# Attention into two gated layers: the power-of-two scale of x1, from Gram matrices of the values or from x1's own maxima per chunk of tokens

## The chip, the cores and the metric

The kernel runs on one core of one Trainium2 chip. A core has a matrix engine (TensorE, in the rows PE for matmuls and PEld for its weight loads), VectorE (DVE), ScalarE (ACT), GpSimd (POOL) and SyncE (SP), which here only issues transfers. Each engine takes its instructions in a fixed order and waits at one until what it needs is there. SBUF is the working memory, PSUM (8 banks) takes the matmul results. The metric is the device time of one execution in microseconds (us), as the median of three runs.

## The reference, cut to what matters

```python
# attention: 2 batches, 8 heads, 576 tokens, head size 64
out_up    = repeat(softmax(scale * mean4(q) @ mean4(k).T) @ mean4(v), 4)   # pooled by 4 tokens
out_local = softmax(scale * q @ k.T where |i - j| < 4) @ v                 # a narrow band
x1 = (out_up + out_local), as 1152 tokens x 512

# first layer, 512 -> 1536 -> 512
x2 = (silu(x1 @ w_gate) * (x1 @ w_val)) @ w_out

# second layer, 8 experts of 512 -> 1024 -> 512, weighted by a balanced routing table
logits = x2 @ moe2_w_gate
P = exp(logits - logits.max());  8 rounds of row and column normalization
out = sum over e of  P[:, e] * (relu(x2 @ w1[e]) @ w2[e])
```

Inputs are float32 and the weights of the first layer come as 64-bit floats that the kernel converts itself. Large products are done in three float16 matmuls each: an operand is scaled by a power of two and split into a high and a low float16 half.

## The kernel before

The work stands in one long program; a scheduler fixes each engine's order before the run, from priorities (mostly the order in which the code is written) and its own idea of durations. It is fully unrolled, so every instruction has one place in its engine's row.

**Attention** (`attention`, L332) goes through 16 heads, two of them (a pair) in one 128-partition tile; pairs 0 to 3 are batch 0, pairs 4 to 7 batch 1. For a head, `scores` (L360) does the score matmuls (tiles `s`, L365 to L374), maxima on DVE (`stm`, `nb`), seven exponentials on ACT (`ex`, L386 to L391) and the division on POOL (L397 to L401); `turn` (L404) transposes on PE (tiles `t`) and copies on ACT (`at`). `combine` (L421) multiplies a pair with its values (tiles `o`, L430 and L438), ACT takes the pooled part out (`avd`, L441), and DVE adds both into `x1` (L444): 128 features x 576 tokens. Scores run four heads ahead of the turns. The tiles `s`, `t` and `o` take two banks each from a ring of six.

**The scale.** x1 is split into `xhl` (high and low half) by `split` (L160): ACT writes the high part, DVE the low part, both times a power of two `s`. Before, `s` is known early: `load_va` (L308) loads a second copy of the values (8 transfers of 288 KB), `x1_scale` (L314) multiplies each 128-column piece with itself on PE (40 matmuls into the tile `vv`), and the largest entry bounds the values. `allmax` with `short` (L153) takes a maximum over the partitions by PE (one transposing matmul), DVE (a reduce) and PE again (a broadcasting matmul, tile `sm`); `pow2` makes the scale in four small DVE operations. Each pair is split in `combine` as soon as its x1 is there.

**First layer.** The 1152 tokens are two chunks, `CH = ((0, 256), (512, 320))`: chunk 0 is tokens 0 to 511 (all of batch 0 but its last 64), chunk 1 is tokens 512 to 1151. For each of 12 blocks f of hidden features, `prep_gv(f)` (L200) loads 1 MB, converts it (`cvg`, L190 to L197), takes its magnitude sum on ACT (L206), its scale by `allmax` (tile `sm_gv`), and splits it into the weight tile `gv`. `gv_step(c, f)` (L487) does the products: for chunk 0 24 matmuls of 512 columns, for chunk 1 48 of 320 columns. For f below 3 on chunk 0 ("early") the results lie in single banks of the pool `psg` (tag `y`, two banks) and pass tanh on ACT and three DVE operations (L515 to L517); later blocks use other banks. The `sm` tiles of `allmax` come from the same two banks, and the two are handed out in the order of the code. Chunk 1 follows chunk 0 by 3 blocks.

`prep_gv(0)` and `prep_gv(1)` are placed among the heads (PREP_AT). From then on each preparation is tied to a step (L640):

```python
with tc.issue_after(gv_done[0, f - 1].ins) if f else nullcontext():
    prep_gv(f + np_)          # np_ = 2
```

so `prep_gv(3)` may not start before the last DVE operation of `gv_step(0, 0)`, `prep_gv(4)` not before that of `gv_step(0, 1)`. Behind the first layer stand `w_out`, the routing and the eight experts (`h_step`, `y_step`), which take most of the run.

Of the kernel before, what the change touches and what calls it, by code (L numbers as in the profile page):

```python
# [22 lines left out]
P = 128  # L23
# [31 lines left out]
@with_exitstack  # L55
def tile_kernel(ctx, tc, qT, kT, vw, vd4, va, wgv, wo, wg2, w1, w2, out):
    nc = tc.nc
# [14 lines left out]
    def tmp(n, nm):  # L72
        return wp.tile([P, 16], F32, tag="tmp", bufs=56, name=nm)[:, :n]
# [86 lines left out]
    def split(hi, lo, src, s, pool=False):  # L160
        if pool:
            A.activation(src, src, AF.Copy, scale=s)
            return A.copy(hi, src), G.tensor_tensor(lo, src, hi, op=ALU.subtract)
        return (A.activation(hi, src, AF.Copy, scale=s),  # L164
                V.scalar_tensor_tensor(lo, src, s, hi, op0=ALU.mult, op1=ALU.subtract))  # L165
# [138 lines left out]

    vas = []
    x1s = []

    def load_va():  # L308
        for i in range(B * NPAIR):
            t = mp.tile([P, 2 * CH[1][1]], F32, tag="xT", bufs=4, name=f"va{i}")[:, :S]  # L310
            nc.sync.dma_start(t, va[i])
            vas.append(t)

    def x1_scale():  # L314


        ps = psg.tile([P, 512], F32, tag="y", name="vv")[:, :P]
        for i, t in enumerate(vas):
            b = t.bitcast(BF16)[:, 1::2]
            for lo in (0, P, 2 * P, 4 * P, 3 * P):  # L320
                n = min(P, S - lo)
                T.matmul(ps[:n, :n], lhsT=b[:, lo:lo + n], rhs=b[:, lo:lo + n],
                         start=(i, lo) == (0, 0), stop=(i, lo) == (B * NPAIR - 1, 3 * P))
        mx = tmp(1, "mxv")
        V.tensor_reduce(mx, ps, axis=AX.X, op=ALU.max)
        m = tmp(1, "mv")
        V.tensor_scalar(m.bitcast(U32), allmax(mx, 1, "v", True).bitcast(U32), 0x7F800000, 1, op0=ALU.bitwise_and,
                        op1=ALU.logical_shift_right)
        V.tensor_scalar(m.bitcast(U32), m.bitcast(U32), float(127 << 22), None, op0=ALU.add)
        x1s.extend(pow2(m, 1, "x1", room=4.0))  # L330

    def attention():  # L332
# [3 lines left out]

        qd, kd, exs, ats = {}, {}, {}, {}

        def pooled(pr):
# [81 lines left out]
        def combine(pr):  # L421
# [21 lines left out]
            for i, (lo, hi) in enumerate(((0, base), (base, S))):  # L443
# [3 lines left out]
                                op=ALU.add)  # L447
            b, k = pr // NPAIR, pr % NPAIR
            o = slice(b * S, (b + 1) * S)
            split(xhl[:, 0, k, o], xhl[:, 1, k, o], x1, x1s[0])  # L450

# [10 lines left out]
        for h in range(AHEAD):  # L462
            start(h)
            if h == 1:
                pooled_v(0)
                x1_scale()
            yield
# [19 lines left out]
    def gv_step(c, f, early):  # L487
# [4 lines left out]
        with tc.high_priority():  # L492
            V.tensor_scalar(iv[:, 0:1], gv_inv[f], x1s[1], 0.5 if early else 1.0, op0=ALU.mult, op1=ALU.mult)
            if early:
                V.tensor_scalar(iv[:, 1:2], iv[:, 0:1], 2.0, None, op0=ALU.mult)
# [135 lines left out]
    load_v(1)  # L631
    load_va()
    for n, _ in enumerate(attention()):
# [148 lines left out]

_INS = ("qT", "kT", "vw", "vd4", "va", "wgv", "wo", "wg2", "w1", "w2")

# [37 lines left out]
```

## Time and profile before

| | us |
|---|---|
| median of 3 runs | 1054.92 |
| lowest and highest | 1052.87, 1056.31 |
| the profiled execution | 1055.02 |
| its span in the trace | 1053.2 |
| PE busy in the span | 1019.6 (97%) |
| DVE, ACT, POOL busy | 767.7, 450.1, 94.3 |

The profile is of one execution, 1.8 us longer than its span and 0.1 us above the median. Times in the trace count from the span's start. The part with attention ends at about 127 us (the last `o` matmul), the first layer follows, and from there to the end PE is the busy engine. A row of a busy table gives time in which an engine worked; what decides the end is the chain of waits, which the profile follows back from the last instruction.

### The profile page before, as it was taken

The numbers are of one execution on the slowest core, as the hardware profiler recorded it, in microseconds if no ns is written. First come the engines' busy times: TensorE is split into PE (matmuls) and PEld (weight loads), VectorE is DVE, ScalarE is ACT, GpSimd is POOL, SyncE is SP. The second block draws the span as 40 slices with busy tenths as digits, with TensorE's granted clock in tenths as the row PEclk, the third lists the DMA queues.
The fourth block names the chain that finished last, engine by engine and source line by source line (L and its number), as shares of the span: only waits on it lengthen the run. The fifth ranks groups of instructions, "written<-read, shape, count | busy, mean of one in ns | idle before, by whom it ended". The sixth has DMA issues, their size and how long they took to land.

```text
span 1053.2 us, 16460 instructions
## 1 busy us (share of the span) xinstructions
PE 1019.6 (97%) x6520; PEld 655.2 (62%) x6521; DVE 767.7 (73%) x1578; ACT 450.1 (43%) x931; POOL 94.3 (9%) x138
## 2 busy tenths in 40 slices
PE   6787998999999999999999999999999999999998
PEld 4676754656567866665756756666575675666644
DVE  7888559887681899878759749758875974984631
ACT  3586656756460656345215414414521541441200
POOL 4786100000000200000000000000000000000000
PEclk9899899999999999999999999999999999999999
DMA  9652132432020022112112100301211110020011
GB/s 263 189 146 52 56 118 85 156 121 81 1 81 1 2 81 80 42 40 81 41 40 79 43 16 26 120 1 41 80 41 40 76 46 17 24 81 1 1 41 51
DMA packets 23614, 67.93 MB, mean 64 GB/s; under 512 B 12208, under 2 KB 12464, under 8 KB 17136
## 3 DMA queue, kind: packets, MB, share of 16 engines
q1 hardware_dynamic: 23536, 66.87, 19.1%
q8 instruction: 51, 0.84, 0.3%
q14 instruction: 27, 0.22, 0.1%
HBM read 64.50 MB, written 2.36 MB: 63 GB/s over the span
## 4 chain that ended last, share of the span: by engine, by line
PE 86%; DVE 6%; ACT 3%; DMA 2%; issue 2%; SPq 0%; POOL 0%; ACTq 0%; DVEq 0%
PE y L172 35%; PE p L172 30%; PE gv L172 8%; PE wo L172 7%; DMA k<-in_kT 2%; PE o L438 2%; ACT ex L386 1%; PE o L430 1%; DVE cvg L196 1%; PE s L368 1%; PE lgps L556 1%; DVE cvg L191 1%; DVE cvg L195 0%; PE t L410 0%; DVE act L528 0%
## 5 line engine op out<-in xcount | busy, mean ns | idle before, releaser
L172 PE MATMUL y<-w,hhl 128*128 128x512 f16 (+1 forms) x1752 | 396.2, 376 | 0.0
L172 PE MATMUL p<-bop,w 128*128 128x320 f16 (+1 forms) x2688 | 354.6, 286 | 0.8 <-DVE u L693 0.7
L172 PEld LDWEIGHTS <-w 128*128 128x128 f16 x2688 | 263.0, 98 | 90.8 <-issue 1.5
L172 PEld LDWEIGHTS <-hhl 128*128 128x128 f16 x1752 | 171.4, 98 | 178.2
L721 ACT ACTIVATE hhl<-h 128x640 f16<-128x640 f32 (+1 forms) x128 | 83.3, 676 | 160.6 <-DVE h L693 160.5
L172 PE MATMUL gv<-xhl,gv 128*128 128x320 f16 (+1 forms) x864 | 145.5, 328 | 6.5 <-ACT gv L164 4.1
L172 PEld LDWEIGHTS <-gv 128*128 128x128 f16 x864 | 84.2, 98 | 62.8 <-issue 5.6
L752 DVE SCALAR_TENSOR_TENSOR acc<-y,pe,acc 128x512 f32<-128x512 f32 (+1 forms) x64 | 47.3, 740 | 101.3 <-PE y L172 100.5
L164 ACT ACTIVATE w<-r,s_w 128x256 f16<-128x256 f32 (+1 forms) x96 | 71.1, 783 | 115.2 <-PE y L172 86.3
L722 DVE SCALAR_TENSOR_TENSOR hhl<-h,hhl 128x640 f16<-128x640 f32 (+1 forms) x128 | 94.6, 754 | 15.2 <-ACT hhl L721 13.7
L693 DVE SCALAR_TENSOR_TENSOR h<-p,u 128x256 f32<-128x256 f32 (+1 forms) x192 | 85.2, 453 | 19.9 <-PE p L172 14.0
L165 DVE SCALAR_TENSOR_TENSOR w<-r,s_w,w 128x256 f16<-128x256 f32 (+1 forms) x96 | 78.2, 834 | 16.8 <-ACT w L164 16.7
L172 PE MATMUL wo<-ahl,wo 128*128 128x320 f16 (+1 forms) x432 | 71.5, 326 | 0.0
L693 DVE SCALAR_TENSOR_TENSOR u<-p,u 128x320 f32<-128x320 f32 (+1 forms) x128 | 57.5, 449 | 4.3 <-PE p L172 3.2
L164 ACT ACTIVATE w<-cmb,s_w 128x512 f16<-128x512 f32 x64 | 43.0, 710 | 40.5 <-DVE cmb L253 37.9
L172 PEld LDWEIGHTS <-wo 128*128 128x128 f16 x432 | 42.3, 99 | 26.9
L151 POOL PARTITION_ALL_REDUCE g_w<-gm_w x16 | 5.9, 372 | 569.1 <-DVE gm_w L147 563.2
L710 ACT ACTIVATE s<-p 128x256 f32<-128x256 f32 (+1 forms) x64 | 25.4, 397 | 56.5 <-PE p L172 56.4
L141 DVE TENSOR_REDUCE mxw<-r 128x1 f32<-128x1024 f32 x32 | 37.5, 1213 | 12.6 <-DMA r<-in_w 12.6
L165 DVE SCALAR_TENSOR_TENSOR w<-cmb,s_w,w 128x512 f16<-128x512 f32 x64 | 46.2, 743 | 0.0
L273 ACT ACTIVATE j<-r 128x1024 f16<-128x1024 f32 x32 | 33.4, 1045 | 26.0 <-DMA r<-in_w 26.0
L693 DVE SCALAR_TENSOR_TENSOR u<-p,s 128x256 f32<-128x256 f32 (+1 forms) x64 | 28.8, 451 | 5.2 <-PE p L172 3.9
(201 smaller groups left out, 952.4 us busy)
## 6 DMA issues: line engine op xcount, KB each, us to landing
r<-in_w SPq DMA_DIRECT2D x32, 1024.0 KB, 5.4
rawg<-in_wgv SPq DMA_DIRECT2D x12, 1024.0 KB, 6.4
rawo<-in_wo SPq DMA_DIRECT2D x6, 1024.0 KB, 4.8
vz<-in_vw SPq DMA_DIRECT2D x16, 160.0 KB, 3.4
k<-in_kT SPq DMA_DIRECT2D x8, 288.0 KB, 6.5
qz<-in_qT SPq DMA_DIRECT2D x16, 144.0 KB, 4.4
v<-in_vd SPq DMA_DIRECT2D x8, 288.0 KB
va<-in_va SPq DMA_DIRECT2D x8, 288.0 KB, 7.7
```

What stands on the lines that cost most here:

```text
L141: V.tensor_reduce(o, i, axis=axis, op=ALU.max, apply_absolute_value=True)
L164: return (A.activation(hi, src, AF.Copy, scale=s), V.scalar_tensor_tensor(lo, src, s, hi, op0=ALU.mult, op1=ALU.subtract))
L165: V.scalar_tensor_tensor(lo, src, s, hi, op0=ALU.mult, op1=ALU.subtract))
L172: T.matmul(ps, lhsT=wf(i, k), rhs=xf(j, k), start=n == 0, stop=n == 3 * nk - 1)
L191: V.scalar_tensor_tensor(f, h, HI_MIN, f, op0=ALU.max, op1=ALU.max)
L273: A.activation(junk, t[:, 2 * j:2 * j + 2].rearrange("p a n -> p (a n)"), AF.Abs, accum_out=mx[:, 2 * i + j:2 * i + j + 1])
L438: T.matmul(dst, lhsT=v[:, w, j], rhs=ats[2 * pr + j][:, w // 4, off:off + hi - lo], start=j == 0, stop=j == 1)
L693: V.scalar_tensor_tensor(o, ps, HSC, u, op0=ALU.mult, op1=ALU.add)
L710: A.activation(s1, p1, AF.Copy, scale=HSC)
L721: ra = A.activation(t[:, 0], h, AF.Relu)
L722: rv = V.scalar_tensor_tensor(t[:, 1], h, 0.0, t[:, 0], op0=ALU.max, op1=ALU.subtract)
L752: V.scalar_tensor_tensor(acc[t][:, ds], ps, p[:, t:t + 1], acc[t][:, ds], op0=ALU.mult, op1=ALU.add)
```

## The change

The second copy of the values, its eight loads, the 40 Gram matmuls and the bound made from them go. Instead, `combine` takes the largest magnitude of each x1 (`absmax`, a DVE reduce of 128x576 into a column of `x1mx`), and when four x1 of a batch are there, `x1_split` makes a scale: a reduce over the columns, `allmax` in its short form, `pow2`. After batch 0 it splits the four x1 for tokens 0 to 511 and copies the last 64 tokens of each into `tail` (ACT); after batch 1 it makes a second scale from all eight columns and splits `tail` and the four x1 of 576 tokens for chunk 1. The four buffers of x1 are held until then. `gv_step` takes the inverse scale of its chunk.

```diff
-    vas = []
-    x1s = []
-    def load_va():
-        for i in range(B * NPAIR):
-            t = mp.tile([P, 2 * CH[1][1]], F32, tag="xT", bufs=4, name=f"va{i}")[:, :S]
-            nc.sync.dma_start(t, va[i])
-            vas.append(t)
-    def x1_scale():
-        ps = psg.tile([P, 512], F32, tag="y", name="vv")[:, :P]
-        for i, t in enumerate(vas):
-            b = t.bitcast(BF16)[:, 1::2]
-            for lo in (0, P, 2 * P, 4 * P, 3 * P):
-                n = min(P, S - lo)
-                T.matmul(ps[:n, :n], lhsT=b[:, lo:lo + n], rhs=b[:, lo:lo + n],
-                         start=(i, lo) == (0, 0), stop=(i, lo) == (B * NPAIR - 1, 3 * P))
-        mx = tmp(1, "mxv")
-        V.tensor_reduce(mx, ps, axis=AX.X, op=ALU.max)
...
-        x1s.extend(pow2(m, 1, "x1", room=4.0))
+    x1i = {}
+    def x1_split(b, x1):
+        mx = x1mx[:, :(b + 1) * NPAIR]
+        s, x1i[b] = pow2(allmax(mx, (b + 1) * NPAIR, f"x1{b}", True), 1, f"x1{b}")
+        n = CH[1][0] if b == 0 else S
+        if b:
+            o = slice(CH[1][0], S)
+            split(xhl[:, 0, :, o], xhl[:, 1, :, o], tail, s)
+        for k, t in enumerate(x1):
+            o = slice(b * S, b * S + n)
+            split(xhl[:, 0, k, o], xhl[:, 1, k, o], t[:, :n], s)
+            if b == 0:
+                A.copy(tail[:, k], t[:, n:])
...
-            b, k = pr // NPAIR, pr % NPAIR
-            o = slice(b * S, (b + 1) * S)
-            split(xhl[:, 0, k, o], xhl[:, 1, k, o], x1, x1s[0])
+            absmax(x1mx[:, pr:pr + 1], x1)
+            x1t.append(x1)
+            if len(x1t) == NPAIR:
+                x1_split(pr // NPAIR, x1t)
+                x1t.clear()
...
-            V.tensor_scalar(iv[:, 0:1], gv_inv[f], x1s[1], 0.5 if early else 1.0, op0=ALU.mult, op1=ALU.mult)
+            V.tensor_scalar(iv[:, 0:1], gv_inv[f], x1i[c], 0.5 if early else 1.0, op0=ALU.mult, op1=ALU.mult)
...
-    load_va()
```

The change also moves instructions that it doesn't name. On PE, before, the products of `gv_step(0, 0)` and `gv_step(0, 1)` stand among the heads. Here is the place in pair 3: a transpose of head 8 (`t`), the first matmuls on the weights `gv_476` (f = 0), then scores of head 11 (`s`).

```order
L374 MATMUL s_1_848<-kd_842,qd_841 72x144 x2
L410 MATMUL t_0_878<-ident,ex_617 128x128 x4
L155 MATMUL sm_gv_1342<-ident,mxg_1340 1x128
L172 LDWEIGHTS gv_476
L172 MATMUL gv_0_00_1361<-xhl,gv_476 128x512
...
L411 MATMUL t_1_879<-ident,ex_617 128x128
L414 MATMUL t_1_879<-ident,ex_617 72x72 x4
L365 LDWEIGHTS identb
L365 MATMUL s_0_893<-maskb,identb 128x512
```

In the changed kernel the first `gv` matmul stands here, behind the last pair's `o` (pair 7), the two matmuls of the second scale (`sm_x_1279`) and the first of a weight scale (`sm_gv_1312`, f = 2):

```order
L431 MATMUL o_1_1256<-at_1227,vz_84 128x92
L431 MATMUL o_1_1256<-at_1242,vz_84 128x92
L157 MATMUL sm_x_1279<-ident,gm_x_1277 1x128
L159 MATMUL sm_x_1279<-gr_x_1280,ones 128x1
L157 MATMUL sm_gv_1312<-ident,mxg_1310 1x128
L174 LDWEIGHTS gv_404
L174 MATMUL gv_0_00_1331<-xhl,gv_404 128x512
```

So all 48 matmuls of `gv_step(0, 0)` and `gv_step(0, 1)` that stood among the heads now stand behind the whole attention and behind both scales.

On DVE, before, the end of `gv_step(0, 0)` (`act_0`) and the conversion of f = 3 (`cvg_1396`) lie in the middle of attention, ahead of pair 5's x1:

```order
L516 TENSOR_TENSOR act_0_1360<-act_0_1360,gv_0_00_1361 128x512
L394 TENSOR_SCALAR rs_1052<-sts_90 128x8
L517 SCALAR_TENSOR_TENSOR act_0_1360<-gv_0_10_1374,iv_0_1357,act_0_1360 128x512
L191 SCALAR_TENSOR_TENSOR cvg_1396<-rawg_1394,cvg_1396 128x1024
L395 RECIPROCAL rs_1052<-rs_1052 128x8
L444 TENSOR_TENSOR x_1076<-o_0_1058,avd_1074 128x364
```

In the changed kernel DVE has, behind the last x1 (pair 7, `x_1273`), first the magnitude and the scale of all, then the low halves of chunk 1, the weight scale of f = 2, and only then `act_0` and the conversion of f = 3 (`cvg_1366`):

```order
L143 TENSOR_REDUCE x1mx<-x_1273 128x1
L149 TENSOR_REDUCE gm_x_1277<-x1mx 128x1
L158 TENSOR_REDUCE gr_x_1280<-sm_x_1279 1x1
...
L167 SCALAR_TENSOR_TENSOR xhl<-x_1273,s_x_1285,xhl 128x576
L136 TENSOR_SCALAR u_gv_1317<-sm_gv_1312 128x1
...
L167 SCALAR_TENSOR_TENSOR gv_1301<-cvg_1304,s_gv_1318,gv_1301 128x1024
L511 SCALAR_TENSOR_TENSOR act_0_1330<-gv_0_10_1344,iv_0_1327,act_0_1330 128x512
L193 SCALAR_TENSOR_TENSOR cvg_1366<-rawg_1364,cvg_1366 128x1024
```

With `act_0`, the conversion of f = 3 has moved behind attention, and that of f = 4 (before, among pairs 6 and 7) behind `act_1`. From the conversion of f = 5 on, the rows of both kernels are nearly the same.

## Rows read from the trace of the kernel before

**Rows 1.** The page: busy time and share of the span of PE, and its granted clock in 40 equal slices of the span, in tenths of full speed.
```profile
PE 1019.6 (97%) x6520; PEld 655.2 (62%) x6521; DVE 767.7 (73%) x1578; ACT 450.1 (43%) x931; POOL 94.3 (9%) x138
...
PEclk9899899999999999999999999999999999999999
```

**Rows 2.** Busy time of the engines in stretches behind attention (start:end, length, then busy us and instructions of each engine, granted clock, share of the DMA engines, GB/s).
```profile
127.00:176.00 49.00, 43.62 (x255) 24.20 (x253) 35.16 (x65) 26.90 (x45) 0.73 (x2) 1.00 0.30 108
176.00:600.00 424.00, 422.95 (x2744) 269.44 (x2745) 335.74 (x710) 205.78 (x347) 14.10 (x21) 1.00 0.17 60
600.00:1053.00 453.00, 449.92 (x2790) 272.74 (x2788) 299.82 (x575) 136.28 (x229) 2.80 (x8) 1.00 0.11 41
```

**Rows 3.** The chain of waits in the first 200 us (start, length, what): two waits for loads of k.
```profile
16.54 9.17 DMA k<-in_kT
25.77 9.62 DMA k<-in_kT
```

**Rows 4.** Issues of transfers: the copy of the values (count, size of one, us to landing), and below it the busy table of the first stretch (its last number is the GB/s moved) and of two stretches in it (the third engine is DVE).
```profile
va<-in_va SPq DMA_DIRECT2D x8, 288.0 KB, 7.7
...
0.00:25.00 25.00, 15.30 (x98) 12.40 (x99) 17.48 (x49) 9.14 (x39) 12.09 (x28) 1.00 0.94 263
...
22.00:28.00 6.00, 4.04 (x33) 3.13 (x32) 6.00 (x15) 5.16 (x25) 5.31 (x7) 1.00 1.05 267
28.00:34.00 6.00, 5.53 (x46) 4.27 (x46) 5.32 (x10) 2.92 (x15) 0.95 (x3) 1.00 0.94 216
```

**Rows 5.** DVE in order of time: the reduce of 576 elements per partition that waited for a load of k.
```profile
35.42 0.75 DVE L343 TENSOR_REDUCE kd<-k 128x144 f32<-128x576 f32 x1 [2.10 <-DMA k<-in_kT]
```

**Rows 6.** PE in order of time: the first matmuls of the combines of pairs 1 to 5, and the end of pair 7's with the `gv` matmuls behind it.
```profile
52.40 0.76 PE L430 MATMUL o<-at,vdz 72*128 72x144 f32 x4
...
64.61 0.76 PE L430 MATMUL o<-at,vdz 72*128 72x144 f32 x4 [0.51 <-ACT ex L386]
...
77.92 0.76 PE L430 MATMUL o<-at,vdz 72*128 72x144 f32 x4
...
90.72 1.02 PE L172 MATMUL gv<-xhl,gv 128*128 128x512 f16 x4 [0.87 <-DVE xhl L165]
91.58 0.66 PE L430 MATMUL o<-at,vdz 72*128 72x144 f32 x4
...
105.30 1.33 PE L430 MATMUL o<-at,vdz 72*128 72x144 f32 x4 [4.29 <-ACT ex L386]
...
109.95 1.17 PE L430 MATMUL o<-at,vdz 72*128 72x144 f32 x4
...
126.01 1.25 PE L438 MATMUL o<-at,vz 128*128 128x120 f32 x10
127.09 5.34 PE L172 MATMUL gv<-xhl,gv 128*128 128x512 f16 x24
132.37 0.38 PE L155 MATMUL sm_gv<-ident,mxg 128*1 128x128 f32 x2
...
135.37 0.38 PE L157 MATMUL sm_gv<-gr_gv,ones 1*128 1x1 f32 x2
```

**Rows 7.** Groups of PE instructions between 10 and 127 us: busy us and mean ns of one, then idle time before them.
```profile
L172 PE MATMUL gv<-xhl,gv 128*128 128x512 f16 x48 | 12.2, 379 | 0.9 <-DVE xhl L165 0.9
...
L322 PE MATMUL vv<-va 128*128 128x128 bf16 (+1 forms) x40 | 4.7, 222 | 0.3 <-DMA va<-in_va 0.2
```

**Rows 8.** Granted clock: the busy table of two stretches (the number behind POOL's is the clock, as a share of full speed).
```profile
100.00:106.00 6.00, 1.71 (x12) 1.43 (x11) 6.00 (x14) 2.25 (x13) 1.40 (x2) 0.85 0.00 1
106.00:112.00 6.00, 6.00 (x33) 5.93 (x33) 0.52 (x4) 4.86 (x22) 2.88 (x5) 0.58 0.53 178
```

**Rows 9.** DVE in order of time, behind attention: pair 7's x1, the conversion of f = 4 around it, the split of x1, the weight scale and split of f = 4, and the last DVE operation of `gv_step(0, 2)`.
```profile
125.49 1.22 DVE L191 SCALAR_TENSOR_TENSOR cvg<-rawg,cvg 128x1024 f32<-128x1024 f32 x1
126.74 0.69 DVE L195 TENSOR_SCALAR cvg<-cvg 128x1024 uint32<-128x1024 uint32 x1
127.47 1.23 DVE L196 SCALAR_TENSOR_TENSOR cvg<-rawg,cvg 128x1024 uint32<-128x1024 uint32 x1
128.61 0.82 DVE L444 TENSOR_TENSOR x<-o,avd 128x364 f32<-128x364 f32 x2
129.35 1.22 DVE L197 SCALAR_TENSOR_TENSOR cvg<-rawg,cvg 128x1024 uint32<-128x1024 uint32 x1
130.48 0.81 DVE L165 SCALAR_TENSOR_TENSOR xhl<-x,s_x,xhl 128x576 f16<-128x576 f32 x1
132.78 0.28 DVE L156 TENSOR_REDUCE gr_gv<-sm_gv 1x1 f32<-1x128 f32 x1 [1.49 <-PE sm_gv L155]
...
139.24 1.28 DVE L165 SCALAR_TENSOR_TENSOR gv<-cvg,s_gv,gv 128x1024 f16<-128x1024 f32 x1 [0.28 <-ACT gv L164]
140.44 0.74 DVE L517 SCALAR_TENSOR_TENSOR act<-gv,iv,act 128x512 f32<-128x512 f32 x1
```

**Rows 10.** ACT in order of time in the same stretch: the pooled part, the high half of an x1, the magnitudes and the high half of a weight block.
```profile
127.29 0.29 ACT L441 ACTIVATE avd<-o 128x144 f32<-128x144 f32 x1 [0.96 <-PE o L438]
129.47 0.78 ACT L164 ACTIVATE xhl<-x,s_x 128x576 f16<-128x576 f32 x1 [1.88 <-DVE x L444]
130.60 1.06 ACT L206 ACTIVATE gv<-cvg 128x1024 f16<-128x1024 f32 x1 [0.36 <-DVE cvg L197]
...
138.06 1.14 ACT L164 ACTIVATE gv<-cvg,s_gv 128x1024 f16<-128x1024 f32 x1
```

More of the change, by code (lines that the diff above doesn't have):

```diff
@@ L55, in tile_kernel @@
 @with_exitstack
-def tile_kernel(ctx, tc, qT, kT, vw, vd4, va, wgv, wo, wg2, w1, w2, out):
+def tile_kernel(ctx, tc, qT, kT, vw, vd4, wgv, wo, wg2, w1, w2, out):
     nc = tc.nc
@@ L101, in tile_kernel @@
         G.memset(vdz[i][:, :, 1, :64], 0.0)
+    x1mx = cp.tile([P, B * NPAIR], F32, name="x1mx")
+    tail = ap.tile([P, KD, S - CH[1][0]], F32, tag="tail", bufs=1, name="tail")
     ones = cp.tile([P, P], F32, name="ones")
@@ L303, in load_v @@
         v4s[pr] = v4
-    vas = []
-    x1s = []
-    def load_va():
-        for i in range(B * NPAIR):
-            t = mp.tile([P, 2 * CH[1][1]], F32, tag="xT", bufs=4, name=f"va{i}")[:, :S]
-            nc.sync.dma_start(t, va[i])
-            vas.append(t)
-    def x1_scale():
-        ps = psg.tile([P, 512], F32, tag="y", name="vv")[:, :P]
-        for i, t in enumerate(vas):
-            b = t.bitcast(BF16)[:, 1::2]
-            for lo in (0, P, 2 * P, 4 * P, 3 * P):
-                n = min(P, S - lo)
-                T.matmul(ps[:n, :n], lhsT=b[:, lo:lo + n], rhs=b[:, lo:lo + n],
-                         start=(i, lo) == (0, 0), stop=(i, lo) == (B * NPAIR - 1, 3 * P))
-        mx = tmp(1, "mxv")
-        V.tensor_reduce(mx, ps, axis=AX.X, op=ALU.max)
[L326 to L329, printed above, removed]
-        x1s.extend(pow2(m, 1, "x1", room=4.0))
+    x1i = {}
[11 more added lines that the diff above has]
+                A.copy(tail[:, k], t[:, n:])
     def attention():
@@ L337, in attention @@
         qd, kd, exs, ats = {}, {}, {}, {}
+        x1t = []
         def pooled(pr):
@@ L465, in attention @@
                 pooled_v(0)
-                x1_scale()
             yield
@@ L780, in tile_kernel @@
                     prep_w2(e + 1)
-_INS = ("qT", "kT", "vw", "vd4", "va", "wgv", "wo", "wg2", "w1", "w2")
+_INS = ("qT", "kT", "vw", "vd4", "wgv", "wo", "wg2", "w1", "w2")
 def kernel(**inputs):
@@ L799 @@
     vdn = vp.reshape(B * NPAIR, 2, HS, FAC, P).transpose(0, 2, 1, 3, 4)
-    va = v.reshape(B * NPAIR, P, S)
     g = np.stack([np.asarray(inputs["moe_w_gate"]), np.asarray(inputs["moe_w_val"])]).view(np.uint64)
@@ L808 @@
     w2 = np.asarray(inputs["moe2_w2"]).reshape(E, 2, KF2 // 2, P, DM).transpose(0, 1, 3, 2, 4)
-    laid = dict(zip(_INS, (heads(q), heads(k), vwin, vdn, va, wgv, wo, wg2, w1, w2)))
+    laid = dict(zip(_INS, (heads(q), heads(k), vwin, vdn, wgv, wo, wg2, w1, w2)))
     nc = bacc.Bacc("TRN2", target_bir_lowering=False, num_devices=1)
```

## The prediction

> **What bounds the kernel now.** I read three views in turn. The page first: PE is busy 97% of the span [rows 1]. Then the busy tables by stretch: from 176 us on PE is busy 423.0 of 424 us and 449.9 of 453 [rows 2], so whatever delays the kernel ahead of 176 us is still there at the end, and whatever it saves ahead of 176 us is saved at the end, unless the wait that stands between takes it. Between 127 and 176 us PE still waits (43.6 busy of 49). So the change, all of whose instructions lie ahead of 176 us, is worth what it does to one moment in this stretch. I take the last DVE operation of `gv_step(0, 2)`, at 140.4 us [rows 9]: behind it the two kernels have nearly the same rows on every engine, and what is late there is late for all. The third view is time order around attention: the chain of waits runs through two loads of k, 9.2 and 9.6 us [rows 3], and PE's own row gives the pace of the pairs, 12.2, 13.3, 13.7 and 13.7 us from combine to combine [rows 6].
>
> **Two terms.** The mark lies at E + 13.2 us, where E = 127.3 us is the end of pair 7's last `o` matmul (126.01 + 1.25) [rows 6, 9]. The change moves E (attention has less to do) and the distance from E to the mark (what was done among the heads is now done behind them).
>
> **Term 1, when attention ends.** What goes: the eight loads of `va`, 2.36 MB, at the 263 GB/s of that stretch 9.0 us of the transfer engines [rows 4]; 40 `vv` matmuls, 4.7 us busy; and 48 `gv` matmuls, 12.2 us busy with starts 0.22 us apart [rows 7], with their tanh and DVE work and the conversions of f = 3 and f = 4. What comes: one reduce per pair of 576 elements, 0.75 us by its like [rows 5], and after pair 3 the first scale with four splits in a row.
> The loads: at most the 9.0 us come through, at least nothing. DVE is busy 6.00 and 5.32 of 6 us while the loads of k are waited for [rows 4], with conversions that both kernels have to do there; it stood idle for the load only 2.1 us [rows 5]. I take 2.6, those and the two reduces for `vv` at about 0.28 each, near the lower end: pair 2's combine starts at 62.0 instead of 64.6 us.
> The pairs: from pair 3's to pair 4's combine PE needs 13.7 us, of which 18 `gv` matmuls take 3.9 and one wait 0.87 [rows 6], so 8.9 us is the floor of a pair. The pair from 52.4 to 64.6 us has no `gv` matmul and takes 12.2, with DVE on the conversions of f = 1 and f = 2; that is the upper end. The change takes f = 3 and f = 4 off DVE there and adds 0.75, so I take 10.2, nearer the floor: a head's scores wait for banks that the exponentials of an earlier head hold, which PE's own work does not hide fully. Three pairs give 30.6.
> The first scale: four ACT splits of about 0.75 stand in a row ahead of the next copies of `turn`, and DVE's `u_x`, which waits for a matmul inside pair 4's combine, holds back the division of head 13 behind it. From nothing (hidden by PE) to 3.1 us; I take 2.0.
> The last stretch, 105.3 to 127.3 us, is 22.0 long. 24 `gv` matmuls (5.2) and the two `sm_gv` matmul pairs (0.6) leave it. Its first 4.6 us run at half clock, after PE had waited 4.3 us: four matmuls take 1.33 us against 0.66 [rows 6, 8], and without that wait 2.5 us fall away. Left are 13.7.
> E after = 62.0 + 30.6 + 2.0 + 13.7 = 108.3 us, 19.0 earlier. With all lower ends 55.6 + 26.7 + 0 + 13.7 = 96.0, with all upper ends 64.6 + 36.6 + 3.1 + 16.2 = 120.5.
>
> **Term 2, from E to the mark.** Before, this is 13.2 us. After, I walk down the rows in the order that the changed kernel has. Absent from the trace is only the new chain as a whole; each piece has a like.
> From E: `avd` 0.3, the adds 0.8, `absmax` 0.75, the reduce over columns 0.15, then `sm_x` on PE 0.35, a DVE reduce 0.28, PE again 0.35, the first operation of `pow2` 0.16, with some 0.05 at each hand-over [rows 5, 6, 9, 10]. At E + 3.3 the bank of `sm_x` is free and `gv_0_00` can start; PE has done nothing of weight since E.
> ACT then writes the high half of `tail` (about 0.4) and four halves at 0.75, to E + 7.2; DVE's low halves end at E + 8.0 [rows 9, 10]. Only behind them stands the operation that reads `sm_gv` of f = 2, and its bank is the one that `gv_0_10` needs: these 12 matmuls start at E + 8.15 and end at E + 10.8, though PE was free at E + 6.3.
> `act_0` is done at E + 11.75 (0.75 and a hand-over). Now the conversion of f = 3 may start: 1.22, 0.69, 1.23 and 1.22 with starts 1.15, 0.65, 1.15, 1.15 apart, 4.1 us, to E + 15.9; the magnitudes on ACT 1.06; `sm_gv` 0.35; only then, at E + 17.3, `gv_1_00`, since it stands behind that matmul on PE. PE has waited 6.2 us by then, longer than the 4.3 us after which it ran at half clock [rows 8], so I count 4.9 us for its 12 matmuls instead of 2.65. The second half of the scale, 0.3; `pow2`, 0.6; the high half of the weights 1.14, the low half 1.28 [rows 9, 10]: f = 3 is ready at E + 25.7.
> `act_1`, 0.75, and the conversion of f = 4, 4.1, end at E + 30.5; PE does f = 3 meanwhile (24 matmuls, 5.3, to E + 31.0) [rows 6]. Magnitudes 1.06, `sm_gv` 0.35, `gv_2_00` 2.65, the second half of `sm_gv` 0.3: E + 34.9. Before, that half ends at 135.4 + 0.3 and the mark follows about 5 us behind it [rows 6, 9]; so the mark lies at E + 40.
> The bounds: E + 37.6 if the clock holds, E + 43 if `gv_0_00` too runs at half clock and each of some twenty hand-overs takes 0.1 us more than I gave. PE does 21 us of matmuls in these 40 us; the rest is waiting that nothing covers, since the work that covered it, the heads, is over.
>
> **Sum.** The mark comes at 108.3 + 40 = 148.3 us against 140.4: 7.9 us later. Behind it the same rows follow with the same waits, so the end moves by as much: against the profiled execution's 1055.0 us (0.1 above the median) 1062.9. I give 1062.8.
>
> **Rivals.**
> *Attention gives back everything.* If the 9.0 us of the loads come through whole and the pairs run at PE's floor, E comes at 96 to 101 us, and the mark, with the clock held, at 133.6 to 141: time 1048 to 1055.6, not slower. It decides from E = 100.4 (100.4 + 40 = 140.4) down. For it speaks that both k loads stand whole in the chain [rows 3] and that DVE is relieved; against it DVE's busy share in just that stretch [rows 4], and that three things must go best at once. Inside this case about 1053 is likeliest.
> *PE's own work sets the time.* The 40 `vv` matmuls leave PE, the `gv` matmuls cost the same wherever they stand, and what is prepared late is hidden. Then 4.7 us go [rows 7], two more `sm_x` pairs of 0.6 to 0.7 us come, and the time is 1055.0 - 4.7 + 1.3 = 1051.6. For it speaks the 97% [rows 1]; against it that PE stood idle or slow around 16 to 46 us anyway, and that the walk above finds 19 us of waits. The Trainium skill (Perfetto Trace Analysis, Identifying Performance Opportunities) has the rule behind this rival: improving a kernel generally means improving its most-contended engine. The trace agrees with it from 176 us on, not in attention.
> *The heads fall behind as well.* The four held x1 buffers and the block of splits in pair 4 let the bank ring run dry, pairs stay at 12.2 us: E = 114 to 116, time 1069 to 1071. For it speaks that DVE operations next to POOL's are stretched in the trace and gain nothing from the change; against it the relief of DVE.
> That the change doesn't do what it says, and some `gv` work still fills the heads' gaps, is ruled out by PE's order.
>
> **How the numbers follow.** Slower as worked out, 1056 to 1069: 0.68. Attention gives back everything, 1048 to 1056: 0.14. PE's own work: 0.08. Heads behind, 1069 to 1072: 0.10. The predicted time is that of the first. The range goes from 1052.5 to 1069: the first case and most of the second, with 2 in 10 outside. A measurement of this kernel tells about 0.3%, 3.2 us, from no change. Faster by more: the third case and a third of the second, 0.12. Within: the rest of the second and 0.05 of the first, 0.15. Slower: 0.63 and 0.10, 0.73.
>
> **What would show it.** Right: the last `o` matmul of attention ends near 108 us; behind it PE waits some 3 us for the scale, then 2, then about 6 ahead of `gv_1_00`, there named as a wait for ACT or for the magnitudes of f = 3; the granted clock dips in that stretch; the last DVE operation of `gv_step(0, 2)` comes near 148. The k loads no longer stand in the chain. Wrong: E near 100 us or below, or no wait over 3 us between E and E + 30, or a time from 176 us on in which PE's work is not the same.

## The result, and the profile after

The changed kernel takes 1068.45 us (median of four runs, 1065.62 to 1069.76), 1.0137 of the kernel before, interval 1.0117 to 1.0157: slower, as forecast, by 12 to 17 us where 7.9 were forecast. The profiled execution took 1069.76 us, its span is 1068.0. Second runs of the same kernel gave 1068.45 again and 1.0145 (1.0123 to 1.0166).

The page, busy time of PE and its granted clock in 40 slices:

```profile
PE   4798699999999999999999999999999999999998
...
PEclk9799899899999999999999999999999999999999
```

PE's busy sum, 1021.2 us, is that of before within 1.6 us [rows 1]; the time is in its waits and in slow matmuls. PE in order of time: the first matmuls of the combines of pairs 2 to 5, the end of pair 7's, and what follows to the mark (the rows that answer to [rows 6]):

```profile
64.08 0.76 PE L423 MATMUL o<-at,vdz 72*128 72x144 f32 x4 [0.15 <-ACT ex L379]
...
75.20 1.09 PE L423 MATMUL o<-at,vdz 72*128 72x144 f32 x4 [2.09 <-ACT ex L379]
...
85.99 0.76 PE L423 MATMUL o<-at,vdz 72*128 72x144 f32 x4
...
98.56 0.76 PE L423 MATMUL o<-at,vdz 72*128 72x144 f32 x4 [1.74 <-ACT ex L379]
99.15 2.54 PE L431 MATMUL o<-at,vz 128*128 128x124 f32 x12
...
112.56 1.03 PE L431 MATMUL o<-at,vz 128*128 128x120 f32 x8
115.86 0.38 PE L157 MATMUL sm_x<-ident,gm_x 128*1 128x128 f32 x2 [2.27 <-DVE gm_x L149]
...
117.64 3.84 PE L174 MATMUL gv<-xhl,gv 128*128 128x512 f16 x12
...
122.13 2.75 PE L174 MATMUL gv<-xhl,gv 128*128 128x512 f16 x12 [0.34 <-DVE u_gv L136]
131.29 0.59 PE L157 MATMUL sm_gv<-ident,mxg 128*1 128x128 f32 x2 [6.41 <-ACT gv L208]
131.81 5.27 PE L174 MATMUL gv<-xhl,gv 128*128 128x512 f16 x12
...
146.81 0.38 PE L157 MATMUL sm_gv<-ident,mxg 128*1 128x128 f32 x2 [1.23 <-ACT gv L208]
```

Attention ends at E = 112.56 + 1.03 = 113.6 us (127.3 before). Behind it PE waits 2.27 us for the scale and 6.41 us for the magnitudes of f = 3, and the 12 matmuls behind each wait take 3.84 and 5.27 us where 12 of the kind take 2.75. DVE in the same stretch, with the low halves in a row, `act_0`, the conversion of f = 3 behind it, and the mark (the rows that answer to [rows 9]):

```profile
119.01 3.00 DVE L167 SCALAR_TENSOR_TENSOR xhl<-x,s_x,xhl 128x576 f16<-128x576 f32 x4
...
124.94 0.74 DVE L511 SCALAR_TENSOR_TENSOR act<-gv,iv,act 128x512 f32<-128x512 f32 x1
125.60 1.22 DVE L193 SCALAR_TENSOR_TENSOR cvg<-rawg,cvg 128x1024 f32<-128x1024 f32 x1
...
140.45 0.74 DVE L511 SCALAR_TENSOR_TENSOR act<-gv,iv,act 128x512 f32<-128x512 f32 x1
...
154.88 0.75 DVE L511 SCALAR_TENSOR_TENSOR act<-gv,iv,act 128x512 f32<-128x512 f32 x1
```

The mark is at 154.9 us, 14.4 later, and the span is 14.8 longer. From the mark to the end of the span it is 912.8 us before and 913.1 after: for these two kernels, what is late at the mark is late at the end. In the second profile of the changed kernel the mark is at 152.9 us and the span is 1066.1 us, 12.5 and 12.9 us above before.

### The profile page after: what moved, and what is told of

Read it like the earlier page. It is cut to its first block, busy times and chain, and to the rows that moved or that the text cites. A ratio compares the mean times of both kernels' runs of the same rounds, so it can differ in the third digit from the quotient of the medians.

```text
span 1068.0 us, 16399 instructions
## 1 busy us (share of the span) xinstructions
PE 1021.2 (96%) x6485; PEld 652.2 (61%) x6485; DVE 776.7 (73%) x1591; ACT 451.1 (42%) x936; POOL 89.8 (8%) x138
## 4 chain that ended last, share of the span: by engine, by line
PE 86%; DVE 7%; ACT 4%; issue 2%; DMA 1%; SPq 0%; POOL 0%; ACTq 0%; DVEq 0%
PE y L174 35%; PE p L174 30%; PE gv L174 11%; PE wo L174 7%; PE o L431 1%; ACT ex L379 1%; DVE cvg L198 1%; DVE xhl L167 1%; PE lgps L550 1%; PE o L423 1%; PE s L361 1%; DVE cvg L199 1%; ACT gv L208 1%; DMA vz<-in_vw 0%; DMA k<-in_kT 0%
## 5 line engine op out<-in xcount | busy, mean ns | idle before, releaser
L174 PE MATMUL gv<-xhl,gv 128*128 128x320 f16 (+1 forms) x864 | 148.7, 335 | 5.8 <-ACT gv L166 4.0
L166 ACT ACTIVATE w<-cmb,s_w 128x512 f16<-128x512 f32 x64 | 43.0, 710 | 40.5 <-DVE cmb L255 37.9
L143 DVE TENSOR_REDUCE mxw<-r 128x1 f32<-128x1024 f32 x32 | 37.5, 1213 | 12.2 <-DMA r<-in_w 12.2
```

The lines of the kernel that those rows point to most:

```text
L143: V.tensor_reduce(o, i, axis=axis, op=ALU.max, apply_absolute_value=True)
L166: return (A.activation(hi, src, AF.Copy, scale=s), V.scalar_tensor_tensor(lo, src, s, hi, op0=ALU.mult, op1=ALU.subtract))
L174: T.matmul(ps, lhsT=wf(i, k), rhs=xf(j, k), start=n == 0, stop=n == 3 * nk - 1)
```

## The experiments

E is the end of attention's last `o` matmul, "way" the time from E to the start of the last DVE operation of `gv_step(0, 2)`, both in the profiled execution. Ratios are to the kernel before on the same chip; the runs were on several chips, so gains between two runs are taken from the ratios unless the two stood side by side. A second run of a kernel stands behind a slash.

| run | median us | ratio (95%) | E | way |
|---|---|---|---|---|
| before | 1054.92 | | 127.3 | 13.2 |
| changed / changed_again | 1068.45 / 1068.45 | 1.0137 (1.0117 to 1.0157) / 1.0145 (1.0123 to 1.0166) | 113.6 / 111.6 | 41.3 / 41.3 |
| old_late_max | 1066.22 | 1.0132 (1.0110 to 1.0155) | 108.5 | 41.5 |
| late_max_own_rings | 1058.55 | 1.0045 (1.0028 to 1.0063) | 125.5 | 17.3 |
| own_rings | 1053.41 | 1.0007 (0.9992 to 1.0022) | 113.9 | 22.8 |
| no_tie | 1064.91 | 1.0114 (1.0095 to 1.0133) | 117.0 | 30.7 |
| own_rings_no_tie | 1048.02 | 0.9951 (0.9937 to 0.9965) | 123.7 | 14.0 |
| old_no_tie | 1053.00 | 1.0004 (0.9990 to 1.0017) | 127.3 | 3.0 |
| old_no_va | 1051.78 | 0.9987 (0.9975 to 0.9998) | 123.1 | 14.7 |
| fill_pe / fill_again | 1066.15 / 1065.02 | 1.0121 (1.0089 to 1.0153) / 1.0111 (1.0090 to 1.0132) | 111.7 / 111.5 | 38.4 / 38.4 |
| first_const / first_const_again | 1067.47 / 1066.05 | 1.0137 (1.0100 to 1.0174) / 1.0124 (1.0104 to 1.0145) | 110.8 / 110.9 | 40.5 / 40.0 |
| late_weights | 1068.27 | 1.0145 (1.0120 to 1.0170) | 111.8 | 41.3 |
| best_late_weights | 1060.08 | 1.0071 (1.0045 to 1.0097) | 125.8 | 6.4 |
| keep_clock | 1075.24 | 1.0212 (1.0193 to 1.0231) | 118.3 | 42.1 |

**One late maximum in the old kernel.** The scheduler hands out the buffers of a ring in the order of the code. The bank of `sm_x` and the small tiles of the second scale (`gm`, `gr`, `u`, `s`, from a ring `tmp`) come in the code ahead of those of `prep_gv(2)` and of the first products. This run adds to the old kernel such a chain and nothing else.

```diff
             split(xhl[:, 0, k, o], xhl[:, 1, k, o], x1, x1s[0])
+            if pr == B * NPAIR - 1:
+                mx = tmp(1, "mxl")
+                absmax(mx, x1)
+                V.tensor_copy(tmp(1, "mxc"), allmax(mx, 1, "late", True))
```

> The kernel before with its loads, Gram matrices and early scale, and one thing added: behind pair 7's x1 a maximum of it over all partitions, whose result nothing reads. Theory (order): that alone puts all gv matmuls behind attention; E near 111 to 118, the way from E to the mark 34 to 38 us (nothing of the late splits in it), mark at 147 to 154, time 1062 to 1068. Rival (the late scale and its block of splits cost the time): no more than 1 to 2 us for one short chain, 1054 to 1057.

1066.22 us. PE behind attention's end:

```profile
110.60 0.58 PE L155 MATMUL sm_late<-ident,mxl 128*1 128x128 f32 x2 [2.08 <-DVE mxl L141]
...
112.69 5.05 PE L172 MATMUL gv<-xhl,gv 128*128 128x512 f16 x12
...
127.46 0.59 PE L155 MATMUL sm_gv<-ident,mxg 128*1 128x128 f32 x2 [6.41 <-ACT gv L206]
127.97 4.24 PE L172 MATMUL gv<-xhl,gv 128*128 128x512 f16 x12
```

The same wait of 6.41 us, slow matmuls behind both waits again and a way of 41.5 us, in a kernel that still loads `va`, has its Gram matmuls and splits early. The late splits aren't needed for the loss. The time lies in the theory's range by luck: E came earlier than forecast (108.5 us for 111 to 118) and the way was longer (41.5 for 34 to 38). The way did not shrink without the late splits because `u_gv` waited for the slow `gv_0_00` instead (5.05 us here, 3.84 in the changed kernel).

**The changed kernel with rings of its own for the second scale.** The bank comes from attention's ring, the four small tiles from buffers of their own.

```diff
+        if late:
+            return ap.tile([P, 16], F32, tag=f"late_{nm}", bufs=1, name=nm)[:, :n]
         return wp.tile([P, 16], F32, tag="tmp", bufs=56, name=nm)[:, :n]
...
+        if late:
+            ps = psa.tile([P, 512], F32, tag="att", bufs=6, name=f"sm_{nm}")
+        else:
+            ps = psg.tile([P, 512], F32, tag="y", name=f"sm_{nm}")
```

(`late` is set around the second scale.) Neither edit was run alone, so which of the two rings holds the `gv` matmuls is not shown.

> The changed kernel, but the second scale takes its bank from attention's ring and its small tiles from a ring of their own; nothing of the computation changes. Theory (order): the first 24 gv matmuls and the preparation of f = 2 and f = 3 return among the heads, the end of attention E goes from 113.3 to 116 to 121 us, the way from E to the last DVE operation of gv_step(0, 2) shrinks from 42 to 15 to 22 us, and the time falls by 10 to 20 us to 1048 to 1058. Rival (attention is what is late: the splits in a block and the held x1): E goes up by as much as the way behind it shrinks, 1065 to 1069.

1053.41 us. The whole loss is gone, 13.7 us by the ratios (1.0137 to 1.0007). PE behind E (113.9 us):

```profile
114.15 2.76 PE L181 MATMUL gv<-xhl,gv 128*128 128x512 f16 x12
...
117.16 0.38 PE L164 MATMUL sm_x<-ident,gm_x 128*1 128x128 f32 x2
117.47 2.76 PE L181 MATMUL gv<-xhl,gv 128*128 128x512 f16 x12
...
128.62 0.38 PE L164 MATMUL sm_gv<-ident,mxg 128*1 128x128 f32 x2 [2.80 <-ACT gv L215]
...
171.08 19.13 PE L181 MATMUL gv<-xhl,gv 128*128 128x512 f16 x98 [4.06 <-ACT gv L173]
```

PE goes from the last `o` straight into `gv_1_00` at full speed, since `gv_step(0, 0)` was done among the heads, and E is little later for it (113.9 against 113.6 and 111.6). The old order is not back as a whole: the 24 matmuls of `gv_step(0, 0)`, the low half of f = 2's weights and the conversion of f = 3 stand among the heads again, the 24 of `gv_step(0, 1)` still behind them. E came earlier and the way is a little longer than the theory had (113.9 us for 116 to 121, 22.8 for 15 to 22).

**Control.** The old kernel's late maximum, from rings of its own in the same way.

> Control for the run with the kernel before and a late maximum: the same late maximum, but its bank comes from attention's ring and its small tiles from a ring of their own. Theory (it was the order in which the two rings hand out their buffers, not the chain): the gv matmuls stand among the heads again and the loss is gone, 1052 to 1056. Rival (the chain or its place in the rows of DVE and PE cost the time): 1060 to 1067.

1058.55 us, outside both ranges. Two thirds of the loss go (1.0132 to 1.0045), with the order. The rest, 4.7 us, is about what the chain costs by its place in PE's row, behind the last `o` and ahead of `gv_2_00`; no run moves the chain alone:

```profile
129.61 0.58 PE L162 MATMUL sm_late<-ident,mxl 128*1 128x128 f32 x2 [4.11 <-DVE mxl L145]
130.04 0.58 PE L162 MATMUL sm_gv<-ident,mxg 128*1 128x128 f32 x2
130.55 3.96 PE L179 MATMUL gv<-xhl,gv 128*128 128x512 f16 x12
```

PE waits 4.11 us there, and the 12 matmuls of `gv_2_00` take 1.2 us more than the 2.75 us at full speed. Before, the 24 matmuls of f = 3 ran in this place [rows 6]; their weights are ready here too (low half done at 118.1 us), but they stand behind the wait. In own_rings `sm_x` stands behind `gv_1_00` and waits for nothing.

**The tie of the preparations.** `prep_gv(3)` and `prep_gv(4)` freed from the steps, in the changed kernel, in own_rings and in the old kernel.

```diff
-            with tc.issue_after(gv_done[0, f - 1].ins) if f else nullcontext():
+            with tc.issue_after(gv_done[0, f - 1].ins) if f > 2 else nullcontext():
```

> The changed kernel without the tie of prep_gv(3) and prep_gv(4) to the steps (later ties stay). Theory: PE's 6.4 us wait ahead of gv_1_00 goes since f = 3 is converted among the heads, the half clock behind it too (2.5 us), f = 4 still waits for the buffer of f = 2; mark 6 to 12 us earlier, 1056 to 1062. Rival (the heads pay for it, since DVE converts f = 3 among them): E later by 4 us, 1062 to 1066. Rival (the rings of banks and small tiles hold the matmuls whatever the ties are, and the waits only change their name): 1067 to 1069.

> The changed kernel with the second scale on rings of its own, and without the tie of prep_gv(3) and prep_gv(4). Theory (the order is all that is left to win): the wait of 2.8 us ahead of gv_2_00 goes and f = 4 is converted before attention's end; mark from 137.4 to 133 to 135.5, 1048 to 1052. Rival (DVE converts among the heads and E is later by as much): 1053 to 1057.

> The kernel before without the tie of prep_gv(3) and prep_gv(4), nothing else; tells whether the version with own rings and no tie is faster by the late scale or by the tie alone. Theory (in the old order act_0 is done at 97 us, the tie holds little there; what the better version gains is the absence of loads and Gram matmuls and the late conversion together): 1051 to 1055. Rival (the tie alone makes the gain): 1046 to 1050.

In the changed kernel 2.4 us come back by the ratios (1.0137 to 1.0114; 3.3 against the second run's 1.0145), short of the theory, and 1064.91 us lies in the first rival's range; the intervals of the three runs overlap. The wait of 6.41 us is gone, but E is 3.4 us later than in the first profile, since DVE converts f = 3 among the heads, and the `gv` matmuls still stand behind it. On own rings 5.9 us come back (1.0007 to 0.9951), and this version, 1048.02 us, is faster than both kernels. I had put the place wrong: the mark is not earlier (137.7 against 136.7). The last of PE's long waits, 4.06 us above, is 0.99 here:

```profile
170.47 1.04 PE L181 MATMUL gv<-xhl,gv 128*128 128x512 f16 x4 [0.99 <-ACT gv L173]
```

The old kernel gains nothing from the same edit (1.0004), though its mark comes 10 us earlier (130.3 us against 140.4). In its order PE has next to no wait there to lose (27.2 us busy of the 28 between 127 and 155 us before), and PE's long wait behind that, 4.1 us before, stays (4.4). So where the ties are changed the mark no longer tells the end.

**What the change removes, alone.** The old kernel without loads and Gram matmuls.

```diff
-    load_va()
...
+        m = tmp(1, "mv")
+        V.memset(m, 4.0)
+        x1s.extend(pow2(m, 1, "x1", room=4.0))
```

> The kernel before without the loads of va and the Gram matmuls; the scale of x1 is a constant, so the bound from the values is left out of the computation. Prices what the change removes, alone. Theory (the freed transfers go to weights, whose conversions then come ahead of the heads' work on DVE): attention gains 0 to 3 us, 1051 to 1055. Rival (the 9.0 us of transfers come through): 1045 to 1048.

1051.78 us: 1.4 us by the ratio (0.2 to 2.6), inside the theory's range. In its profile E is 4.1 us earlier than before and the way 1.5 us longer.

**The slow clock.** Matmuls that nothing reads, 24 behind attention's last `o` and 20 behind `act_0`, in PE's two waits.

```diff
+                fill(avd, 24, "a")
...
+                fill(act[0, 0], 20, "b")
```

> The changed kernel with matmuls on PE that nothing reads: 24 of 144 columns behind attention's last matmul and 20 of 512 columns ahead of the magnitudes of f = 3, where PE waits 2.3 and 6.4 us. Theory (the half clock behind the waits is 1.1 us of gv_0_00 and 2.5 us of gv_1_00, and both lie on the chain): both tiles take 2.75 us, mark 3 to 4 us earlier, 1063 to 1066. Rival (the clock costs nothing there, or the added matmuls stand in the way): 1067 to 1070.

> The kernel with matmuls on PE that nothing reads, unedited, with more rounds beside the changed kernel. Theory (half clock behind the two waits lies on the chain; its first look had 38.4 us from E to the mark against 41.3): 2 to 4 us below the changed kernel. Rival (executions differ by as much, the clock is worth nothing here): 0 to 1 us below.

The first run left it open by its interval; the second, with the changed kernel beside it, has 1065.02 (1063.63 to 1065.55) against 1068.45 (1066.85 to 1069.41), 3.4 us. PE in the second:

```profile
115.18 2.76 PE L174 MATMUL gv<-xhl,gv 128*128 128x512 f16 x12
...
119.87 2.75 PE L174 MATMUL gv<-xhl,gv 128*128 128x512 f16 x12 [1.62 <-DVE u_gv L136]
129.03 0.38 PE L157 MATMUL sm_gv<-ident,mxg 128*1 128x128 f32 x2 [0.90 <-ACT gv L208]
129.34 2.76 PE L174 MATMUL gv<-xhl,gv 128*128 128x512 f16 x12
```

Both tiles run at full speed. Of the first one's 1.1 us a wait for `u_gv` takes the place (1.6 us instead of 0.3; it stands behind the low halves on DVE); the second one's 2.5 us come through. From E to the mark it is 2.9 us less.

**The block of the first scale.** Chunk 0 scaled by a constant, pair by pair.

> The changed kernel, but chunk 0 is scaled by a constant, pair by pair as its x1 is there (the first maximum is left out of the computation); the second scale and its rings are as changed. Prices the block of the first scale in attention. Theory (the block costs what the changed kernel's step from pair 4's to pair 5's combine has over that of the old kernel with the late maximum, 12.6 against 8.8 us): E from 113.3 to 108.5 to 110.5, the way behind it the same 42 us, 1064 to 1066. Rival (the block is hidden, E is late because the weights are converted earlier): E at 112 to 114, 1067 to 1069.

> The kernel with the constant first scale (the first maximum is left out of the computation), unedited, with more rounds beside the changed kernel. Theory (the block of splits costs 3 us of attention, the step from pair 4's to pair 5's combine being 9.5 against 12.6 us, and they reach the end): 2 to 4 us below the changed kernel. Rival (other steps of attention give it back): 0 to 1.5 us below.

1067.47 us and a ratio of 1.0137, the same as the changed kernel's, which is the rival's value; then 1066.05 (1065.40 to 1066.90) beside the changed kernel's 1068.45 (1066.85 to 1069.41), 2.4 us, the theory's, with ratios whose intervals overlap. So what the block costs at the end is not settled, between nothing and 2.4 us. In attention it shows: the step from pair 4's to pair 5's combine is 9.5 us in both profiles with the constant and 12.6 in both of the changed kernel. The rows of the changed kernel show what it is, DVE and then ACT around pair 4:

```profile
89.56 0.16 DVE L136 TENSOR_SCALAR u_x<-sm_x 128x1 f32<-128x1 f32 x1 [1.49 <-PE sm_x L159]
...
90.89 2.26 DVE L167 SCALAR_TENSOR_TENSOR xhl<-x,s_x,xhl 128x512 f16<-128x512 f32 x2 [0.17 <-ACT xhl L166]
...
94.40 1.19 DVE L167 SCALAR_TENSOR_TENSOR xhl<-x,s_x,xhl 128x512 f16<-128x512 f32 x1
...
96.08 0.73 DVE L167 SCALAR_TENSOR_TENSOR xhl<-x,s_x,xhl 128x512 f16<-128x512 f32 x1
96.74 0.15 DVE L373 TENSOR_TENSOR nb<-stm,scl 128x4 f32<-128x4 f32 x1
```

```profile
90.14 2.56 ACT L166 ACTIVATE xhl<-x,s_x 128x512 f16<-128x512 f32 x4
97.00 0.37 ACT L379 ACTIVATE ex<-s,nb 128x128 f32<-128x128 f32 x1 [3.39 <-DVE nb L373]
```

The four low halves on DVE, 4.2 us with their stretching, stand ahead of the next head's `nb`, and ACT's exponentials wait 3.39 us for that. The high halves on ACT, 2.56 us, are done before that wait begins.

**Where the freed loads went.** The loads of k of 9.2 and 9.6 us [rows 3] are gone from the chain of waits of the changed kernel, as forecast, and yet its combine of pair 1 comes at 54.6 us (53.0 in the second profile) against 52.4 before [rows 6]. Pair 2's comes at 64.1 us (65.9 in the second profile) against 64.6. Two causes were tried: the granted clock, and weights that are converted ahead of the heads. DVE's rows show the second: the conversion of f = 2, which before lies around and behind pair 2's combine, is done ahead of it in the changed kernel. The first and last of its four DVE operations, before and after:

```profile
62.96 0.69 DVE L194 TENSOR_SCALAR cvg<-cvg 128x1024 f32<-128x1024 f32 x1
...
69.67 1.21 DVE L197 SCALAR_TENSOR_TENSOR cvg<-rawg,cvg 128x1024 uint32<-128x1024 uint32 x1
```

```profile
44.96 1.89 DVE L196 TENSOR_SCALAR cvg<-cvg 128x1024 f32<-128x1024 f32 x1 [0.47 <-ACT cvg L195]
...
52.24 1.21 DVE L199 SCALAR_TENSOR_TENSOR cvg<-rawg,cvg 128x1024 uint32<-128x1024 uint32 x1
```

```diff
+                if h in GF:
+                    gram(ld[GF[h]], 20)
```

(keep_clock: 20 matmuls each on the keys of pairs 2 and 3.)

```diff
-            prep_gv(PREP_AT.index(n))
+            with tc.issue_after(nbs[1].ins):
+                prep_gv(PREP_AT.index(n))
```

(late_weights, with f = 2 tied to the maximum of pair 1's x1 in the same way; best_late_weights is own_rings_no_tie with both, and its edit ties f = 3 and f = 4 to that maximum as well.)

> The changed kernel with 40 matmuls of 128 columns on the keys of pairs 2 and 3, whose results nothing reads, where the old kernel had its Gram matmuls. Clock theory (between 22 and 34 us PE is granted 0.69 and 0.50 in the changed kernel and 1.00 in the old one, and the heads' own matmuls there take twice as long): granted clock 1.00 in 22 to 34 us, combine of pair 1 from 53 to 55 us to 50 to 52 us, the time 1064 to 1067. Order theory (the early conversions on DVE make pair 1 late): combine of pair 1 stays at 53 to 55 us, 1067 to 1070.

> The changed kernel with the conversion of f = 0 and f = 1 on DVE behind the maxima of head 1, as in the kernel before, and that of f = 2 behind the maximum of pair 1's x1. Order theory (weights that come earlier are converted earlier, ahead of the heads' maxima): combine of pair 1 from 53 to 55 us to 50 to 52 us, E from 111.6 to 113.6 us to 108.5 to 110.5 us, 1064 to 1066. Clock theory (PE at half clock sets the pace there): combine of pair 1 stays at 53 us or later, 1067 to 1069.

> The version with own rings and no tie, with the conversions of f = 0 to f = 2 as late as in the run beside it. Order theory: E 2 to 3 us earlier than 123.7 us, 1045 to 1047. Rival (what attention wins PE waits for behind it, since f = 2 is ready later): 1047 to 1050.

keep_clock, 1075.24 us, outside both ranges, tells nothing of the two causes. PE in it:

```profile
21.37 1.68 PE L455 MATMUL gram<-k 128*128 128x128 bf16 x20 [4.30 <-DMA k<-in_kT]
...
35.14 2.31 PE L455 MATMUL gram<-k 128*128 128x128 bf16 x20 [6.65 <-DMA k<-in_kT]
```

The added matmuls waited for the keys and held the heads behind them. late_weights, PE, and its busy table for the stretches of [rows 4] (the last but two is the clock):

```profile
50.60 0.76 PE L426 MATMUL o<-at,vdz 72*128 72x144 f32 x4 [0.91 <-ACT ex L382]
...
61.45 0.66 PE L426 MATMUL o<-at,vdz 72*128 72x144 f32 x4
...
72.92 0.76 PE L426 MATMUL o<-at,vdz 72*128 72x144 f32 x4 [2.47 <-ACT ex L382]
```

```profile
22.00:28.00 6.00, 1.89 (x14) 1.48 (x15) 6.00 (x13) 2.73 (x15) 5.55 (x7) 0.84 0.48 129
28.00:34.00 6.00, 2.93 (x12) 2.02 (x12) 6.00 (x10) 4.22 (x21) 6.00 (x6) 0.50 0.28 68
```

The combine of pair 1 comes at 50.6 us instead of 53.0 to 54.6, as the order theory said, with the clock as low as in the changed kernel's second profile (0.82 and 0.50 there), so the slow clock in these two stretches is not what makes it late. The time is no shorter for it, 1068.27, the clock theory's value: E is at 111.8. The conversion of f = 2 now falls behind pair 2's combine (11.5 us from pair 2 to pair 3, with a wait of 2.47), and the lead on the changed kernel's second profile shrinks from 4.5 us at pair 2's combine to 3.1 at pair 3's and 0.9 at pair 4's. In the version without ties the edit costs 12.6 us by the ratios (0.9951 to 1.0071), which neither theory had. There DVE has the four small operations of the second scale between conversions of later weights (the scale is done at 137.3 us, the first of the four starts at 134.1), ACT's splits and its next activation stand behind the scale, and PE waits 4.8 us for that activation and later 4.1 us for a weight block.

## Why the prediction was right behind attention and wrong inside it

**Direction and place: right.** Slower, because what was done among the heads is done behind them, with waits that nothing covers. own_rings shows it as the cause: 24 `gv` matmuls and two preparations back among the heads, the rest of the change kept, and 13.7 us are back. old_late_max shows the reverse.

**Term 2, from E to the mark: right.** 40 us forecast, 41.3 and 41.3 measured, with the stations of the walk (`gv_0_00` at E + 4.0 for 3.3, `gv_0_10` at 8.5 for 8.15, `gv_1_00` at 18.2 for 17.3, the conversion of f = 4 done at 32.0 for 30.5). The wait ahead of `gv_1_00` is 6.41 us for 6.2, the 12 matmuls behind it 5.27 us for 4.9. That `gv_0_00` runs slow too (3.84 us) was in the upper bound only.

**Term 1, when attention ends: the step that failed.** E was to be 108.3 us; it is 113.6, in the second profile 111.6. What failed in both profiles is the first term, the loads: "at least nothing", "I take 2.6". Pair 2's combine was to come at 62.0 us and comes at 64.1 and, in the second profile, here:

```profile
65.92 0.66 PE L423 MATMUL o<-at,vdz 72*128 72x144 f32 x4
```

Against 64.6 before that is 0.5 us gained and 1.3 lost. It comes at 62.2 to 64.6 us in the four profiles with the copy of the values (before, old_late_max, late_max_own_rings, old_no_tie), and at 64.1 to 68.9 in the ten without it that leave the weights as early as they get and add nothing to the heads. The term took the transfers for the only thing that moves. But the weights come earlier too, and DVE converts them ahead of the heads' maxima: the first operation on f = 0 starts at 18.4 us instead of 21.9, the first on f = 2 at 45.0 instead of 63.0. With these held back (late_weights) pair 2's combine comes at 61.5. Busy tables of the changed kernel and of the old one without `va`, for the stretches of [rows 4] (the third engine is DVE, the number behind POOL's the clock):

```profile
22.00:28.00 6.00, 2.15 (x10) 1.42 (x11) 6.00 (x11) 2.88 (x12) 5.96 (x7) 0.69 0.56 143
28.00:34.00 6.00, 2.20 (x10) 1.79 (x9) 6.00 (x12) 3.04 (x17) 4.15 (x4) 0.50 0.56 212
```

```profile
22.00:28.00 6.00, 1.73 (x9) 1.30 (x9) 6.00 (x10) 3.10 (x13) 6.00 (x7) 0.66 0.48 124
28.00:34.00 6.00, 2.20 (x11) 1.48 (x10) 6.00 (x13) 2.83 (x17) 4.52 (x5) 0.50 0.69 232
```

DVE is full, 6.00 of 6 us, in both. [Rows 4] showed DVE's share and I named it as the reason to stay near the lower end, but still gave 2.1 us of idle time to the change; old_no_va prices the whole removal at 1.4 us, and there pair 2's combine comes at 68.7, so what it gains it gains behind that. The upper end of the pairs was misread as well: the conversions of f = 1 and f = 2, which I put into the step from 52.4 to 64.6 us, lie almost wholly outside it (DVE ends the first at 41.4 us and does the second from 62.96 to 70.9, rows above).

The first profile has 3.2 us more, which the second doesn't repeat. One part is the three pairs with the first scale, 34.5 us for 32.6 (the steps from combine to combine are 11.1, 10.8 and 12.6 for 10.2, 10.2 and 12.2; in the second profile 10.1, 9.2 and 12.6). The step with the scale's block is right in size in both, for the wrong reason: I costed it at ACT's splits and at `u_x`, and it is DVE's low halves ahead of `nb`. The other part is the last stretch, 15.0 for 13.7: PE waits 1.74 us ahead of pair 5's combine, and the 12 matmuls behind it take 2.54 us instead of 1.50. In the second profile PE waits 1.74 us there too, the 12 take 1.50, and the stretch is 13.9.

**The range.** 1052.5 to 1069 holds the median by half a microsecond, but 1.0137 of 1054.92 is 1069.4. I had the bound of E at 120.5 us in the text and cut the range at 1069, against the rival in which the heads fall behind (E at 114 to 116), to which 113.6 is nearer than to 108.3; its reason, pairs that stay at 12.2 us, is not what happened. With both upper ends, 120.5 + 43, the mark is at 163.5 us and the time at 1078. The range reached 10.3 us below the forecast and 6.2 above it, and the lower side rested on gains in attention that no row had shown.

**The rivals.** "Attention gives back everything" fails with E. "PE's own work sets the time" fails: PE's work is 1.6 us from that of before, the time 13 to 15. The Trainium skill (Perfetto Trace Analysis, Optimization Strategy) has, beside the rule that I cited, one that fits: where the most contended engine changes from stage to stage, interleaving the stages may help. The trace agrees in part: from 176 us on PE is the busy engine, while in attention no engine is full throughout (PE 81.0, DVE 77.7 and ACT 69.5 us busy of the 100 between 10 and 110 us in the changed kernel), the old order interleaved the two stages and the changed one doesn't; own_rings, which interleaves half of the 48 matmuls again, is 13.7 us below the changed kernel.

What stays open: whether PE's slow clock between 22 and 34 us costs the heads anything by itself (late_weights shows only that pair 1's combine can come early with it), and what the first scale's block costs at the end.

## What to carry to other kernels

Before costing a new reduction by its instructions, ask which rings its buffers come from and what stands behind it in them: in old_late_max a chain of five small operations at the end of a stage put 48 large matmuls of the next stage, and what was left of its preparations, behind that stage. Work that covers another stage's waits is worth its cover, not its busy time, so a change that separates two stages has to be costed by walking the rows that are left alone. And before transfer time is counted as gained, ask what is loaded in its place and which engine works on that: here the weights came earlier, DVE converted them earlier, and 9.0 us of transfers and 4.7 us of matmuls less were worth 1.4 us. Where such a doubt is named, the bound of the range has to move with it, not only the estimate.

## What the runs showed of the hardware

PE's granted clock falls also inside a stage when its work is thinned: between 28 and 34 us it is 1.00 with 5.53 us of matmuls [rows 4] and 0.50 with 2.20 us. Behind a wait of 6.41 us the next 12 matmuls took 5.3 us in the changed kernel, 4.2 in old_late_max, 4.7 and 3.9 in the two of first_const, against 2.75 at full speed: behind the same wait they differ by up to 1.4 us from kernel to kernel and by 0.8 us between two profiles of one kernel (first_const). Work that nothing reads, put into the waits, gave 3.4 us of it back.
